# Operand sums cast one turn later, six blocks carried into the first block unit, and weight-conversion steps set by stage

## The chip, the core and the metric

The kernel runs on one core of a Trainium2 chip. The metric is device microseconds (us) of one execution; lower is better. The engines that matter here are PE (TensorE: matrix products, into PSUM), DVE (VectorE) and ACT (ScalarE), and SP, whose queue issues all the DMA of the stretch in question. Each engine runs its own instructions strictly in the order in which they stand in its program, and waits when the next one's inputs or buffers are not there yet.

## What is computed

Local attention with block summaries (8 heads, 2 batches, 768 positions), then a token and channel mixer, then a second channel mixer with a layer norm in front. The change touches the last two parts:

```python
u = x + h.transpose(0, 2, 1)                          # after the token mixer
x = u + np.maximum(u @ w_ch1, 0.0) @ w_ch2            # first layer:  512 -> 1536 -> 512
xn = (x - mu) / np.sqrt(var + 1e-06) * g_ln
out = x + np.maximum(xn @ w_ch1, 0.0) @ w_ch2         # second layer: 512 -> 2048 -> 512
```

All is in float32. Weights arrive as 64-bit numbers. They are decoded on the core to float32, and each float32 matrix is split in a high and a low part, so that a product is three matrix multiplications (high by high, high by low, low by high; `mm3`, lines 275 to 277).

## The kernel before

**Weight conversion.** The weights come in 62 pieces, called halves (512 columns of all 128 partitions each). A generator, `conversion`, handles one half after the other: an SP load into one of 3 stage buffers (L168), an absolute value on ACT (L115, tile `dec`), four bit operations on DVE (L129, L131, L133, L137), then the split: a cast on ACT for the high part and a subtraction on DVE for the low part. The first 30 halves stay in SBUF, in tiles called slots. The other 32 belong to the second layer: they are split into a spill buffer (tile `sp`, or `sps` for the sums of four blocks; casts on ACT at L186 to L190 and L250, subtractions on DVE at L210 to L220 and L255) and written back to DRAM by an SP DMA. There are two spill buffers, used in turn, so the cast of one spill waits until the write of the spill before the last one has landed. `convert_all(n)` advances the generator by n steps; a step is about one DVE operation.

**First layer.** The 1536 rows are taken in 4 groups of 3 row tiles and 12 chunks (key c = 3 to 14). A unit is one chunk of one group: `g3` (12 multiplications of 384 columns into a PSUM bank of the pool `ps_mm`, then ReLU: `ah` on ACT, L624, and `al` on DVE, L625) and, one unit later, `g4` (three blocks of three 512-column multiplications into the group's accumulators). There are 48 units, n = 0 to 47: first 24 for groups 0 and 1, then 24 for groups 2 and 3. After each unit the kernel before calls `convert_all(5)`. Background work runs between the blocks of `g4`: `start(1)` advances a background generator, `finish()` ends what was started. Both together are called a turn here. The transposition of the rows (`transpose_u`, tiles `tu` and `xt`) is such work. `ps_mm` has two banks, which `g3`, the transposes and the second layer's products share in turn.

**Operands of the second layer.** `prep_x` normalizes a row group (ACT, tile `xn`, L554), transposes it on PE (tile `tx`, L585), scales it on ACT (tile `f`), makes the sums T1 to T4 on DVE, and casts each operand into its high and low parts (`split`, L572 on ACT, L573 on DVE). Eight turns make the operands of one half of the rows. Those for the first half are made from n = 38 on, those for the second half in block units 2 to 5.

**Second layer.** 16 block units follow (`unit`, 8 for each half of the rows). Each makes seven products of block sums (k = 0 to 6, two `mm3` of 384 columns each, operands B11, T2, B21, T1, B22, T3, T4), combines them on DVE (tiles `sm`, `um`, `wm`, L686; the first is a copy on ACT, L696), applies ReLU (L677, L678) and leaves twelve second-matrix blocks (`second`), which the next unit places between its own products. The blocks that a unit gets are spread over its seven products: as many at each as are left, divided by the products left, rounded up. `step(k)` follows each product: it advances the conversion by 2 or 3 steps and runs background turns. Weights are loaded from DRAM into rings that lie in the slots of the first layer.

**What sets the order.** From n = 10 on, ACT's order is that of the code; from the block units on, PE's too. The order on DVE and SP, and on PE in the first layer, is made by a scheduler that places instructions by estimates of its own, so an edit in one place moves instructions in others.

## Time and profile before

| | |
|---|---|
| runs | 596.69, 599.54 and 600.32 us; median 599.54 us |
| profiled execution | 596.65 us, its span 594.5 us |
| PE busy | 569.3 us, 96% of the span |
| DVE busy | 407.8 us, 69% |
| ACT busy | 256.8 us, 43% |
| DMA | 121.07 MB, mean 204 GB/s |
[...]

The span runs from the first to the last instruction; 2.15 us of the execution lie around it. The profile has a line of 40 slices in which PE is almost always at 9 (90% or more), with lower digits in the attention part at the front and in slices 23 and 25 (327 to 342 us and 357 to 372 us). Durations of matmuls are modelled and overlap: what one multiplication occupies is read from the distance of two starts.

### The profile page before, as it was taken

The page shows a single profiled execution, that of the slowest core. Times are in us where ns is not written, and L with a number is a line of the kernel's source. Part 1 is how long each engine was busy: PE and PEld are TensorE (multiplying, and loading weights), DVE is VectorE, ACT ScalarE, POOL GpSimd, SP SyncE. Part 2 cuts the span into 40 slices and gives each one's busy share as a digit, 9 for nine tenths or more (in the row PEclk, how much of TensorE's full clock was granted, in tenths as well). Part 3 has the DMA queues.
Part 4 walks back from the last instruction along what each step waited for, and adds up shares of the span by engine and source line. Part 5 has one row for each costly group of instructions (what it writes and reads, how often), then busy time and mean ns, then how long its engine had stood idle before and what let it go on. Part 6 is the DMA issues. An engine that isn't in the chain of part 4 may idle for free.

```text
span 594.5 us, 9756 instructions
## 1 busy us (share of the span) xinstructions
PE 569.3 (96%) x3488; PEld 491.6 (83%) x3488; DVE 407.8 (69%) x992; ACT 256.8 (43%) x559; POOL 44.2 (7%) x78
## 2 busy tenths in 40 slices
PE   7878999999999999999999797999999999999997
PEld 3456777788999889999889686888889989898896
DVE  4799997995399799786799898854543644333334
ACT  3889888442144345243885334544311111111110
POOL 1555622000000000000000000000000000000000
PEclk8998999999999999999999898999999999999999
DMA  8999930344044467687589988865656775565412
GB/s 281 340 279 300 279 107 4 106 142 142 1 145 171 140 249 240 230 299 253 187 266 332 293 314 305 311 219 174 191 181 192 231 226 179 182 190 182 140 35 107
DMA packets 51206, 121.07 MB, mean 204 GB/s; under 512 B 5075, under 2 KB 11475, under 8 KB 51158
## 3 DMA queue, kind: packets, MB, share of 16 engines
q1 hardware_dynamic: 51152, 120.43, 62.2%
q8 instruction: 28, 0.46, 0.3%
q14 instruction: 20, 0.16, 0.1%
q10 hardware_dynamic: 6, 0.02, 0.0%
HBM read 94.21 MB, written 26.21 MB: 203 GB/s over the span
## 4 chain that ended last, share of the span: by engine, by line
PE 79%; DVE 7%; DMA 7%; ACT 5%; issue 1%; SPq 1%; ACTq 0%; DVEq 0%
PE acc_x L276 7%; PE acc_x L277 7%; PE acc_x L275 7%; PE m L275 6%; PE m L276 6%; PE m L277 6%; DMA stage<-in_wts_dram 4%; PE g L275 2%; DMA w2s<-sp 2%; PE g L277 2%; PE g L276 2%; ACT pr L391 2%; PE av L418 1%; DVE dec L133 1%; PE pt L398 1%
## 5 line engine op out<-in xcount | busy, mean ns | idle before, releaser
L276 PE MATMUL acc_x<-slot,ah 128*128 128x512 f32 x192 | 76.0, 396 | 0.0
L275 PE MATMUL acc_x<-slot,ah 128*128 128x512 f32 x192 | 75.9, 395 | 0.0
L277 PE MATMUL acc_x<-slot,al 128*128 128x512 f32 x192 | 75.9, 395 | 0.0
L677 ACT ACTIVATE ah<-sm 128x384 fp32r<-128x384 f32 x32 | 16.8, 524 | 109.4 <-DVE sm L686 109.4
L275 PE MATMUL m<-slot,slot 128*128 128x384 f32 x126 | 44.1, 350 | 1.1 <-ACT sm L696 0.4
L137 DVE SCALAR_TENSOR_TENSOR dec<-stage,dec 128x512 uint32<-128x512 uint32 x62 | 44.5, 718 | 0.5
L115 ACT ACTIVATE dec<-stage 128x512 f32<-128x512 f32 x62 | 41.6, 674 | 7.6 <-DMA stage<-in_wts_dram 7.6
L133 DVE SCALAR_TENSOR_TENSOR dec<-stage,dec 128x512 uint32<-128x512 uint32 x62 | 43.5, 702 | 0.6
L277 PEld LDWEIGHTS acc_x<-slot,al 128*128 128x128 f32 x192 | 36.3, 189 | 8.1
L276 PE MATMUL m<-slot,slot 128*128 128x384 f32 x126 | 43.0, 342 | 0.0
L277 PE MATMUL m<-slot,slot 128*128 128x384 f32 x126 | 43.0, 341 | 0.0
L276 PEld LDWEIGHTS acc_x<-slot,ah 128*128 128x128 f32 x192 | 36.5, 190 | 4.1
L275 PEld LDWEIGHTS acc_x<-slot,ah 128*128 128x128 f32 x192 | 36.5, 190 | 3.8
L391 ACT ACTIVATE pr<-sn,mn 128x120 f32<-128x120 f32 x96 | 30.6, 385 | 5.7 <-DVE mn L381 5.3
L686 DVE TENSOR_TENSOR um<-m,sm 128x384 f32<-128x384 f32 x16 | 8.9, 557 | 28.9 <-PE m L277 28.6
L129 DVE TENSOR_SCALAR dec<-dec 128x512 f32<-128x512 f32 x62 | 27.2, 441 | 2.0 <-ACT dec L115 2.0
L275 PEld LDWEIGHTS m<-slot,slot 128*128 128x128 f32 x126 | 24.0, 190 | 5.1 <-DVE um L686 1.3
L678 DVE SCALAR_TENSOR_TENSOR al<-sm,ah 128x384 fp32r<-128x384 f32 x32 | 17.8, 557 | 13.0 <-ACT ah L677 13.0
L131 DVE TENSOR_SCALAR dec<-dec 128x512 uint32<-128x512 uint32 x62 | 26.3, 424 | 0.4
L276 PEld LDWEIGHTS m<-slot,slot 128*128 128x128 f32 x126 | 24.0, 191 | 2.0
L361 PE MATMUL scores<-K,Q 64*64 64x120 f32 x384 | 16.4, 289 | 9.2 <-DVE mn L381 6.2
L686 DVE TENSOR_TENSOR sm<-m,sm 128x384 f32<-128x384 f32 x16 | 8.9, 555 | 23.3 <-PE m L277 23.3
(1392 smaller groups left out, 1490.4 us busy)
## 6 DMA issues: line engine op xcount, KB each, us to landing
stage<-in_wts_dram SPq DMA_DIRECT2D x62, 512.0 KB, 3.7
slot<-w1s SPq DMA_DIRECT2D x94, 256.0 KB, 3.0
slot<-w2s SPq DMA_DIRECT2D x32, 512.0 KB, 4.0
w1s<-sps SPq DMA_DIRECT2D x16, 512.0 KB, 3.6
w2s<-sp SPq DMA_DIRECT2D x16, 512.0 KB, 4.6
V<-in_v_dram SPq DMA_DIRECT2D x16, 306.0 KB, 7.7
extra<-w1s SPq DMA_DIRECT2D x18, 256.0 KB, 3.4
w1s<-sp SPq DMA_DIRECT2D x8, 512.0 KB, 4.1
```

Of the source, the lines that this page charges most:

```text
L115: nc.scalar.activation(m, self.raw[n][:, :, 1].bitcast(F32), AF.Abs)
L129: nc.vector.tensor_scalar(m, m, MAG_LO, MAG_HI, op0=ALU.max, op1=ALU.min)
L131: nc.vector.tensor_scalar(mi, mi, 3, 0x3FFFFFF8, op0=ALU.logical_shift_left, op1=ALU.bitwise_and)
L133: nc.vector.scalar_tensor_tensor(mi, t[:, :, 1], 0xC0000000, mi, op0=ALU.bitwise_and, op1=ALU.bitwise_or)
L137: nc.vector.scalar_tensor_tensor(mi, t[:, :, 0], 29, mi, op0=ALU.logical_shift_right, op1=ALU.bitwise_or)
L275: nc.tensor.matmul(out, lhs[0], rhs[0], start=first, stop=False)
L276: nc.tensor.matmul(out, lhs[0], rhs[1], start=False, stop=False)
L277: nc.tensor.matmul(out, lhs[1], rhs[0], start=False, stop=last)
L391: nc.scalar.activation(pr[:, u], sn[:, u], AF.Exp, bias=mn[:, u : u + 1], scale=-1.0)
L677: nc.scalar.activation(ah, x, AF.Relu)
L678: nc.vector.scalar_tensor_tensor(al, x, 0.0, f32(ah), op0=ALU.max, op1=ALU.subtract)
L686: add = lambda o, x, y: nc.vector.tensor_tensor(o, x, y, op=ALU.add)
```

## The change

Four edits.

1. `prep_x` gets one more turn in front, in which only the first normalization stands, and the casts of the sums T1 to T4 are kept in a list and made one turn later, after the next turn's scaling and normalization. Both preparations take nine turns instead of eight; the second is queued one block unit earlier, so that its first turn falls in block unit 1.
2. `g4` returns its three blocks as functions. The last unit (n = 47) doesn't run the blocks of chunk 13 but hands them on, together with those of chunk 14: block unit 0 gets six blocks instead of the three of chunk 14 that it ran behind its first product, and spreads them over its first six products.
3. The steps after a unit are 5 for n below 10, 6 for n = 10 to 23, 5 for n = 24 to 38 and 4 for n from 39; in the block units each product is followed by 2 steps instead of 2 and 3 in turn.
4. The weight loads for ring places 9 to 11 move from the first to the last product of block unit 0. In block unit 1, nine turns instead of eight.

```diff
 # prep_x
         self.normalize(2 * s + seq[0][2], seq[0][0] + 2 * seq[0][1])
-        f, t = {}, {}
+        yield
+        yield
+        f, t, wait = {}, {}, []
...
                 self.normalize(2 * s + ni, ne + 2 * nh)
+            for k, v in wait:
+                self.split(s, *k, v)
+            wait = []
...
-                self.split(s, "T1", e, t["T1"])
+                wait.append((("T1", e), t["T1"]))
...
-                self.split(s, "T3", e, t["T3"])
-                self.split(s, "T2", e, t["T2"])
+                wait.append((("T3", e), t["T3"]))
+                wait.append((("T2", e), t["T2"]))
...
-                self.split(s, "T4", e, t["T4"])
+                wait.append((("T4", e), t["T4"]))
             if n + 1 == len(seq):
+                for k, v in wait:
+                    self.split(s, *k, v)
 # g4
-        for j in range(GT):
-            s = slice(j * P, j * P + P)
...
+        return [lambda j=j: self.g4_tile(g, c, a, j, first, last) for j in range(GT)]
+
+    def g4_tile(self, g, c, a, j, first, last):
+        s = slice(j * P, j * P + P)
+        acc = self.acc[g % 2 * GT + j]
+        self.mm3(acc, (a[0][:, s], a[1][:, s]), self.half[2 * c + 1], first, last)
+        if last:
+            us = self.u[:, g * GT + j]
+            self.nc.vector.tensor_tensor(us, acc, us, op=ALU.add)
+        self.finish()
+        self.start(1)
 # run, first layer
             if (s, f, g) == (1, 5, 3):
-                later += [self.prep_x(0)] * 8
+                later += [self.prep_x(0)] * 9
...
-                self.g4(*prev)
+                blocks = self.g4(*prev)
+                if n == len(units) - 1:
+                    pending += blocks
+                else:
+                    for fn in blocks:
+                        fn()
...
-            self.convert_all(5)
+            self.convert_all(5 if n < 10 or 24 <= n < 39 else 6 if n < 24 else 4)
 # run, block units
-        pending = deque([lambda: self.g4(*prev)])
+        pending += self.g4(*prev)
...
-                if n == 0 and k == 0:
+                if n == 0 and k == 6:
                     for r in range(9, RING):
                         self.load_w1(r)
-                self.convert_all(2 + k % 2)
+                self.convert_all(2)
                 if n == 1 or n in range(2, 6) and k in (1, 5):
-                    for _ in range(2 if (n, k) == (1, 6) else 1):
+                    for _ in range(2 if n == 1 and k > 4 else 1):
...
-            if n == 2:
-                self.bg += [self.prep_x(1)] * 8
+                self.bg += [self.prep_x(1)] * 9
```

The order of the instructions moves in three places that the prediction speaks of. A row gives the line, the operation, the tile written and the tiles read.

**Place 1, ACT, where the first layer goes from groups 0 and 1 to groups 2 and 3.** `ah_('u', 1)_14` is the last ReLU of group 1, `ah_('u', 2)_3` the first of group 2, the `xt` casts empty the transposes of group 3. Before:

```order
L624 ACTIVATE ah_('u', 1)_14_2658<-g3_('u', 1)_14_2645 128x384
L514 CAST xt2_69<-tu_3_0_2665 128x384
L514 CAST xt2_69<-tu_3_1_2674 128x384
L186 CAST sp34_2687<-dec34_2597 128x2x256
L115 ACTIVATE dec36_2689<-stage36_2603 128x512
L624 ACTIVATE ah_('u', 2)_3_2712<-g3_('u', 2)_3_2699 128x384
L514 CAST xt2_69<-tu_3_2_2683 128x384
```

After:

```order
L631 ACTIVATE ah_('u', 1)_14_2687<-g3_('u', 1)_14_2674 128x384
L514 CAST xt2_69<-tu_3_0_2694 128x384
L514 CAST xt2_69<-tu_3_1_2703 128x384
L250 CAST sps1_0_2717<-sa1_2669 128x2x256
L250 CAST sps1_1_2719<-sb1_2670 128x2x256
L190 CAST sp36_2725<-dec36_2595 128x512
L115 ACTIVATE dec38_2727<-stage38_2627 128x512
L631 ACTIVATE ah_('u', 2)_3_2744<-g3_('u', 2)_3_2731 128x384
L514 CAST xt2_69<-tu_3_2_2712 128x384
```

The conversion stands one half and a half further on there. Between the two ReLUs, where one spill cast (`sp34`) stood, there now stand the two casts of sums (`sps1_0`, `sps1_1`) and behind them the next spill cast, `sp36`, which takes the buffer of `sps1_0`.

**Place 2, ACT, at the start of block unit 2.** `sm_2` is the copy that frees the PSUM bank of the unit's first product, `xn_2_0` the first normalization for the second half of the rows, `sd_3` a square root of the statistics. Before:

```order
L190 CAST sp57_4130<-dec57_3937 128x512
L115 ACTIVATE dec59_4132<-stage59_3963 128x512
L537 ACTIVATE sd_3_4139<-ve_3_4138 128x3
L696 COPY sm_2_4163<-m0_2_4155 128x384
L186 CAST sp58_4193<-dec58_4081 128x2x256
L115 ACTIVATE dec60_4195<-stage60_4108 128x512
L554 ACTIVATE xn_2_0_4199<-u_137,nb_2_4057,rs_2_4049 128x128 x3
L589 ACTIVATE f1_0_B11_4207<-tx_2_0_4203,gt_140 128x384
```

After:

```order
L190 CAST sp57_4132<-dec57_3921 128x512
L115 ACTIVATE dec59_4134<-stage59_3943 128x512
L537 ACTIVATE sd_3_4138<-ve_3_4137 128x3
L554 ACTIVATE xn_2_0_4152<-u_137,nb_2_4057,rs_2_4049 128x128 x3
L704 COPY sm_2_4166<-m0_2_4158 128x384
L591 ACTIVATE f1_0_B11_4201<-tx_2_0_4197,gt_140 128x384
L554 ACTIVATE xn_3_0_4203<-u_137,nb_3_4150,rs_3_4142 128x128 x3
```

`xn_2_0` moved from behind the spill cast `sp58` to a place in front of the copy `sm_2`; `sp58` moved behind the two of them and further back.

**Place 3, ACT, from the end of the first layer to block unit 0.** `ah_('u', 3)_14` is the last ReLU of the first layer, slots 5 to 9 hold the operands B22, T3, T2, B21 and T4, `sm_0` is the copy after the first product. Before:

```order
L589 ACTIVATE f0_1_B21_3741<-tx_0_3_3734,gt_140 128x384
L572 CAST slot8_1626<-f0_1_B21_3741 128x384
L572 CAST slot9_1627<-t0_1_T4_3745 128x384
L624 ACTIVATE ah_('u', 3)_14_3775<-g3_('u', 3)_14_3762 128x384
L250 CAST sps5_0_3790<-sa5_3758 128x2x256
L250 CAST sps5_1_3792<-sb5_3759 128x2x256
L696 COPY sm_0_3808<-m0_0_3800 128x384
```

After:

```order
L190 CAST sp52_3756<-dec52_3540 128x512
L115 ACTIVATE dec54_3758<-stage54_3590 128x512
L631 ACTIVATE ah_('u', 3)_14_3774<-g3_('u', 3)_14_3761 128x384
L591 ACTIVATE f0_1_B21_3789<-tx_0_3_3785,gt_140 128x384
L572 CAST slot6_1624<-t0_1_T3_3745 128x384
L572 CAST slot7_1625<-t0_1_T2_3746 128x384
L572 CAST slot8_1626<-f0_1_B21_3789 128x384
L572 CAST slot9_1627<-t0_1_T4_3797 128x384
L704 COPY sm_0_3811<-m0_0_3803 128x384
```

Three operand casts (slots 6, 7 and 9) and that of the last transposed block (slot 8) now stand behind the last ReLU, and a spill cast, `sp52`, in front of it; the two casts of sums that stood between are gone from here, they come two units earlier.

## Rows read from the trace of the kernel before

**Rows 1.** Stretches of core 0: us, busy time by engine, clock, DMA share.

```profile
core 0: us, PE busy (x) PEld busy (x) DVE busy (x) ACT busy (x) POOL busy (x), PEclk, DMA share, GB/s
120.00:320.00 200.00, 200.00 (x1024) 180.49 (x1023) 158.78 (x330) 92.47 (x186) 0.00 (x0) 1.00 0.58 196
320.00:366.00 46.00, 39.13 (x174) 33.18 (x174) 42.67 (x104) 19.63 (x41) 0.00 (x0) 0.93 0.93 319
366.00:585.00 219.00, 218.63 (x1090) 196.09 (x1089) 103.40 (x194) 53.62 (x112) 0.00 (x0) 1.00 0.58 184
```

**Rows 2.** PE in order of time: start, us, line, tiles; idle before and releaser.

```profile
321.43 0.33 PE L275 MATMUL m<-slot 128*128 128x384 f32 x1
...
328.26 0.44 PE L275 MATMUL m<-slot,slot 128*128 128x384 f32 x1 [0.35 <-DVE sm L686]
...
331.54 0.44 PE L275 MATMUL m<-slot 128*128 128x384 f32 x1 [0.90 <-DVE sm L686]
...
334.21 0.49 PE L275 MATMUL m<-slot,extra 128*128 128x384 f32 x1 [1.35 <-DVE um L686]
...
336.10 0.63 PE L275 MATMUL acc_x<-slot,ah 128*128 128x512 f32 x1
...
338.73 0.44 PE L275 MATMUL m<-slot,extra 128*128 128x384 f32 x1 [0.27 <-DVE um L686]
...
341.88 0.45 PE L275 MATMUL m<-slot,slot 128*128 128x384 f32 x1 [0.43 <-ACT sm L696]
...
346.85 0.34 PE L275 MATMUL m<-slot,slot 128*128 128x384 f32 x1
...
347.91 0.39 PE L275 MATMUL acc_x<-slot,ah 128*128 128x512 f32 x1
...
349.29 0.34 PE L275 MATMUL m<-slot,slot 128*128 128x384 f32 x1
...
361.58 1.24 PE L585 MATMUL tx<-ident,xn 128*128 128x128 f32 x3 [3.53 <-ACT xn L554]
362.48 0.67 PE L275 MATMUL m<-slot,slot 128*128 128x384 f32 x1
...
364.55 0.63 PE L275 MATMUL acc_x<-slot,ah 128*128 128x512 f32 x1
...
366.24 0.34 PE L275 MATMUL m<-slot,slot 128*128 128x384 f32 x1
```

**Rows 3.** ACT in order of time, at the start of block unit 2.

```profile
357.90 0.46 ACT L696 COPY sm<-m 128x384 f32<-128x384 f32 x1
359.96 0.62 ACT L186 CAST sp<-dec 128x512 fp32r<-128x512 f32 x1 [1.59 <-DMA w2s<-sp]
360.48 0.66 ACT L115 ACTIVATE dec<-stage 128x512 f32<-128x512 f32 x1
361.05 1.25 ACT L554 ACTIVATE xn<-u,nb,rs 128x128 f32<-128x128 f32 x3
```

**Rows 4.** DVE in order of time, end of the first layer and block unit 0.

```profile
320.24 0.55 DVE L625 SCALAR_TENSOR_TENSOR al_('u', 3)_14_3776<-g_('u', 3)_14_3762,ah_('u', 3)_14_3775 128x384 fp32r<-128x384 f32 x1
...
333.59 0.56 DVE L686 TENSOR_TENSOR um<-m,um 128x384 f32<-128x384 f32 x1
```

**Rows 5.** ACT in order of time, the turn to groups 2 and 3.

```profile
217.08 0.48 ACT L514 CAST xt<-tu 128x384 fp32r<-128x384 f32 x1 [0.55 <-PE tu L510]
...
220.68 0.49 ACT L624 ACTIVATE ah_('u', 2)_3_2712<-g_('u', 2)_3_2699 128x384 fp32r<-128x384 f32 x1 [2.03 <-PE g_('u', 2)_3_2699 L277]
```

**Rows 6.** PE and DVE at the same turn.

```profile
222.10 0.40 PE L275 MATMUL acc_('u', 2)_0_2765<-slot,ah_('u', 2)_3_2712 128*128 128x512 f32 x1
...
217.69 0.55 DVE L515 TENSOR_TENSOR xt<-tu,xt 128x384 fp32r<-128x384 f32 x1
```

**Rows 7.** DVE and ACT around 250 us: two spilled sums and the next spill.

```profile
250.88 0.69 DVE L255 TENSOR_TENSOR sps<-sa,sps 128x512 fp32r<-128x512 f32 x1
...
254.43 0.62 ACT L190 CAST sp<-dec 128x512 fp32r<-128x512 f32 x1 [3.06 <-DMA w1s<-sps]
...
255.52 0.47 ACT L624 ACTIVATE ah_('u', 3)_5_3053<-g_('u', 3)_5_3040 128x384 fp32r<-128x384 f32 x1
```

**Rows 8.** DVE and ACT around 321 us: the same pair, and the next spill.

```profile
321.04 0.69 DVE L255 TENSOR_TENSOR sps<-sa,sps 128x512 fp32r<-128x512 f32 x1
...
325.76 0.62 ACT L190 CAST sp<-dec 128x512 fp32r<-128x512 f32 x1 [2.58 <-DMA w1s<-sps]
```

More of the change, by code (lines that the diff above doesn't have):

```diff
@@ L628, in g4 @@
     def g4(self, key, c, a, first, last):
-        nc = self.nc
         g = key[1]
@@ L634, in g4 @@
                 self.acc[i] = self.ps_acc.tile([P, 512], F32, tag=f"acc{i}", name=f"acc_{key}_{j}")
-        for j in range(GT):
-            s = slice(j * P, j * P + P)
-            acc = self.acc[g % 2 * GT + j]
-            self.mm3(acc, (a[0][:, s], a[1][:, s]), self.half[2 * c + 1], first, last)
-            if last:
-                us = self.u[:, g * GT + j]
-                nc.vector.tensor_tensor(us, acc, us, op=ALU.add)
-            self.finish()
-            self.start(1)
+        return [lambda j=j: self.g4_tile(g, c, a, j, first, last) for j in range(GT)]
[8 more added lines that the diff above has]
+        self.start(1)
     def ring_w1(self, n):
@@ L923, in run @@
         order = ctx.enter_context(ExitStack())
-        later = deque()
+        later, pending = deque(), deque()
         for n, (s, f, g) in enumerate(units):
```

## The prediction

> **What bounds the kernel now.** I read four views: the busy time by stretch, PE in order of time, ACT and DVE in order of time around PE's waits, and the order of before and after. The first shows that PE sets the time: it is busy for 200.00 of 200 us up to 320 us and for 218.63 of 219 us from 366 us on, at granted clock 1.00. Only between 320 and 366 us does it stand idle, 39.13 of 46 us busy, with DVE at 42.67 us and clock 0.93 [rows 1]. So no edit can gain anything outside these 46 us, unless it takes work from PE, which none does; and anything that makes PE wait elsewhere is lost at once.
>
> What these 46 us lose follows from PE's own rows [rows 2]. From the first product of block unit 0 (321.43) to the fourth of unit 2 (366.24) are 44.81 us. Undisturbed, a product takes 1.06 us (346.85 to 347.91) and a block 0.69 (347.91 to 349.29 holds two). The stretch holds 17 products (7, 7 and 3) and 21 blocks (3 in unit 0, 12 in unit 1, 6 in unit 2), 18.0 and 14.5 us, and one group of transposes, an estimated 0.4. That is 32.9, so **11.9 us are lost**. Six waits hold 6.83 of it: 0.35, 0.90, 1.35, 0.27, 0.43 and 3.53. [...] From 334.21 to 338.73 stand one product and two blocks, 2.44 undisturbed, and the wait of 0.27; from 361.58 to 366.24 the transposes, a product and two blocks, 2.84 undisturbed. They take 4.52 and 4.66, so the lower level costs 1.8 us each time, 3.6 together. The remaining 1.5 is some 0.25 at each wait, for the pipeline to drain and fill.
>
> [...]
>
> **What the edits do to this stretch.** *The last wait.* The 3.53 us at 361.58 end with ACT's `xn`. ACT has it behind a spill cast that itself waits 1.59 us for a write to land: cast 359.96, absolute value 360.48, `xn` 361.05 [rows 3]. After the change `xn_2_0` stands in front of `sm_2` (357.90) and the spill cast behind both, so it can be done about 2 us before PE wants it: statistics for it are ready, since edit 1 gives it a turn of its own in front. The wait goes (3.53), the low clock behind it (1.8) and the refill (0.25): 5.6 us. What is late next is `sm_2`, by up to `xn`'s 0.57 of ACT; PE has two blocks (1.38) there as cover.
>
> *The waits for DVE.* Between `al` of the last chunk (320.24) and the `um` that frees the bank for unit 1 (333.59) DVE runs 27 instructions, 0.49 each, without a pause worth the name [rows 4]. It is the bound there: PE's work over it is 7 products and 3 blocks, 9.5 us, against 13.3. Edit 2 lays three more blocks between the products: 2.1 us of cover, taken from n = 47, where PE was not waiting. Edit 3 brings the conversion some eight DVE operations ahead by the end of the first layer, and takes 14 instead of 17 steps in a block unit; in the order DVE has 110 instead of 121 instructions from `al` of the last chunk to the third `al` of unit 0's results. Up to the `um` named it is only 26 for 27. So of the 13.3 us some 12.8 remain, against 11.6 of PE work: the wait at unit 1's first product shrinks from 1.35 plus those ahead of it to 1.1 to 2.2, without certainty that the clock holds. Against it, place 3 adds a wait at unit 0's second product, whose operand T2 (slot 7) is now cast behind the last ReLU and behind `f`: 0.4, up to 2 if the write in front of `sp52` lands late. I leave 2.2 us in the stretch (1.8 at unit 1, 0.4 at T2); the waits of units 1 and 2 (0.27, 0.43) go with the eleven DVE instructions fewer (11 × 0.49 = 5.4). **Gain 11.9 − 2.2 = 9.7 us**; bounds 5.6 (the last wait alone) and 11.9.
>
> **What they cost elsewhere.** *Place 1, near 222 us.* Before, ACT writes `xt` of group 3's second transposes at 217.08, then a spill cast and an absolute value, and then waits 2.03 us for PE before the first ReLU of group 2 at 220.68 [rows 5]; PE's block on it starts at 222.10 without a wait [rows 6]. After, two casts of sums and `sp36` stand there, and `sp36` takes the buffer of the first sum, so it waits until that sum has gone to DRAM. The same pair stands near 250 us: DVE's subtraction starts at 250.88, and the next spill cast, after 3.06 us of waiting for the write, at 254.43, that is 3.55 later; the ReLU behind it starts 1.09 after that [rows 7]. Where DMA is busier, the subtraction at 321.04 is followed by the spill cast at 325.76, 4.72 later [rows 8]. At 250 us PE lost nothing, since the ReLU there was not yet needed; at the turn it is, for PE's next block reads it.
>
> [...]
>
> Now the sum. The subtraction for `xt` is at 217.69 [rows 6]; DVE has it, 0.55, and some small statistics ahead of the subtraction of the first sum, which I put at 218.75. Plus 3.55 is 222.3 for `sp36`, plus 1.09 is 223.4 for the ReLU, against 220.68; plus the 1.42 from ReLU to block (220.68 to 222.10) is 224.8. PE would stand 2.7 us at most, and 1.9 if the sum starts 0.4 earlier and the ReLU is followed at once by the block; I take **2.4**, with 4 as upper bound (4.72 instead of 3.55) and 0 as lower (if the scheduler's DVE order lets the sum go ahead of group 3's work). Whether the clock falls behind a single wait of that size no row shows: behind 3.53 and behind three waits of 2.60 in six us it did, behind 0.35 and 0.90 it did not. I charge half of 1.8, **0.9**.
>
> *Costed at nothing.* The casts put off by a turn (edit 1) lie in stretches in which PE doesn't wait [rows 1]; they are the same casts, and what they hide behind is PE's 1.38 us of blocks at each product. What they cost without it is place 3's T2. The nine later loads (edit 4) are needed in the middle of unit 1, some ten us after their issue; they go down SP's queue behind the spill writes. Steps taken from the block units cost nothing as long as the last spilled weights are in DRAM before unit 4 reads them, and the conversion is only five operations behind at unit 2.
>
> **The sum**, on the profiled execution's own time: 596.65 − 9.7 + 2.4 + 0.9 = **590.2**. That execution stands at the low end of the runs (596.69), 2.9 us under their median; I carry half of that, 1.4, and get **591.5**. About 1%, 6 us, is what a measurement of this kernel can tell from no change; the forecast lies just past it.
>
> **Rivals.** *A, the forecast*: most waits go, one new one at 222 us; 588 to 593.5.
>
> *B, the turn costs nothing*: ACT's write lands in time, or DVE does the sum early. For it: 2.03 us of idle ACT stand in front of the ReLU [rows 5]. Against it: 3.55 + 1.09 is more than what lies between 217.69 and 220.68. Then 596.65 − 9.7 = 587.0, or with the whole 11.9 584.8; with the median's 1.4, 586 to 588.4.
>
> *C, the waits only move*: place 3's `sp52` waits for the sums' write as at 325.76, and the ReLU `ah` of the last chunk with it, T2 comes 2 us late and the clock falls there, in unit 0 and at 222 us. Then only the last wait's 5.6 is gained, and 2.4 + 1.8 are paid, with up to 2 more at T2: 595.3 to 597.3, or with the median's 1.4 up to 598.7.
>
> *D, slower*: six steps a unit put spill casts directly in front of ReLUs on ACT throughout n = 10 to 23, not at the turn alone. In each such pair a cast waits for the write 2.58 to 3.06 us [rows 7, 8]; `g3` of a unit gives its ReLU about one unit of slack, so PE pays only when the wait starts late in it. If it pays 2.4 at each of the turn and three other places, 9.6 is paid against 9.7 gained and from the fifth on the change loses: with lowered clock behind each, 600 to 606. Against it: PE waits nowhere before 320 us now although such pairs are there already [rows 1, 7].
>
> **How the numbers follow.** Chances: A 0.50, B 0.12, C 0.30, D 0.08. The likeliest gives 591.5, its own range 588 to 593.5. Leaving out D and the lower part of B leaves 586 to 598. Faster by over 1% (under 593.5) takes A nearly whole, with 0.42, and B's 0.12 less a little for runs that lie high: 0.52. Within 1% takes the rest of A and C less a little: 0.40. Slower: D, 0.08.
>
> **What would show it.** In the trace of the changed kernel: no wait of PE for `xn` at unit 2, and product times of 1.06 us there; one wait of PE for ACT's ReLU of group 2's first chunk near 222 us, with ACT's `sp36` waiting for `w1s<-sps` just ahead; waits of 0.4 us at T2 and 1 to 2 us at unit 1's first product, on DVE; clock 0.97 or more between 320 and 366 us. The prediction is wrong in its gain if PE still waits over 4 us in this stretch, wrong in its cost if the turn shows no wait or more than 4 us, and wrong altogether if PE waits at several chunks between n = 10 and 23.

## The result and the profile after

The changed kernel takes 591.64 us (median of 8 runs) against 599.45 us before (8 runs). The timed ratio is 0.9882, 95% interval 0.9852 to 0.9912; the plain ratio of the two medians, 0.9870, lies inside that interval. The forecast was 591.5.

Busy time of the changed kernel in the stretches of [rows 1] (the columns are those; the last stretch ends 3 us earlier, since the program does):

```profile
120.00:320.00 200.00, 197.84 (x1009) 178.69 (x1010) 160.23 (x332) 89.08 (x178) 0.00 (x0) 1.00 0.58 197
320.00:366.00 46.00, 43.45 (x221) 38.95 (x220) 45.02 (x109) 23.58 (x51) 0.00 (x0) 1.00 0.92 325
366.00:582.00 216.00, 215.41 (x1074) 193.02 (x1073) 103.19 (x193) 53.45 (x112) 0.00 (x0) 1.00 0.59 186
```

PE, which was never idle between 120 and 320 us, now loses 2.16 us there. Between 320 and 366 us it is busy for 43.45 us instead of 39.13, and the clock is 1.00 instead of 0.93. DVE is busier than before, 45.02 of 46 us. (The changed program is some 5 us later there. With the stretch moved along, 324.97 to 370.97 us, PE is busy for 43.30 and DVE for 45.12 us, and the clock is 1.00 again.)

PE of the changed kernel in order of time: three marks (last chunk of group 1, third chunk of group 2, last chunk of group 3), its waits between them and after, and the first transpose in unit 2, to set beside [rows 2]:

```profile
215.82 0.33 PE L275 MATMUL g_('u', 1)_14_2674<-xt,slot 128*128 128x384 f32 x1
...
227.44 0.50 PE L275 MATMUL acc_('u', 2)_0_2797<-slot,ah_('u', 2)_3_2744 128*128 128x512 f32 x1 [2.08 <-ACT ah_('u', 2)_3_2744 L631]
...
232.04 0.34 PE L275 MATMUL g_('u', 2)_5_2821<-xt,slot 128*128 128x384 f32 x1
...
322.22 0.34 PE L275 MATMUL g_('u', 3)_14_3761<-xt,slot 128*128 128x384 f32 x1
...
326.43 0.44 PE L275 MATMUL m<-slot 128*128 128x384 f32 x1 [1.62 <-ACT f_B L591]
...
339.24 0.44 PE L275 MATMUL m<-slot,extra 128*128 128x384 f32 x1 [0.93 <-DVE um L694]
...
359.90 0.49 PE L587 MATMUL tx<-ident,xn 128*128 128x128 f32 x3
360.19 0.44 PE L275 MATMUL m<-slot,slot 128*128 128x384 f32 x1
...
587.28 0.39 PE L277 MATMUL acc_x<-slot,al 128*128 128x512 f32 x1
```

The wait of 3.53 us for `xn` is gone: the transpose at 359.90 starts without one. Three waits of some size are left: a new one of 2.08 us for the first ReLU of group 2, a new one of 1.62 us at unit 0's first product, and 0.93 us at unit 1's. The next longest after 200 us is 0.31 us, at the last product of unit 2.

The same marks before:

```profile
212.73 0.33 PE L275 MATMUL g_('u', 1)_14_2645<-xt,slot 128*128 128x384 f32 x1
...
226.63 0.34 PE L275 MATMUL g_('u', 2)_5_2789<-xt,slot 128*128 128x384 f32 x1
...
590.52 0.39 PE L277 MATMUL acc_x<-slot,al 128*128 128x512 f32 x1
```

So the **turn** (group 1's last chunk to group 2's third) takes 16.22 us instead of 13.90, and the **rest** (from there to the last multiplication) 355.24 instead of 363.89. Together that is 6.33 us less. The two profiled executions are only 3.27 us apart (593.38 and 596.65 us), because the part in front of all the changes was 3.1 us longer in the one of after: the first layer (first multiplication of unit n = 0) starts at 108.42 us there and at 105.34 before. In the fourteen traces of this study that start lies between 105.17 and 109.12 us, whatever the kernel; the edits begin behind it, at n = 10. I therefore compare traces by turn and rest, and whole kernels by the timed ratios. Each kernel has one trace. The turn repeats well: in the eight traces without a wait it takes 13.86 to 13.90 us. How well the rest repeats for one and the same kernel no run shows, so differences of a few tenths in it are not to be read.

### The profile page after: what moved, and what is told of

It is laid out like the page before. It is cut to its first block, busy times and chain, and to the rows that moved or that the text cites. A ratio compares the mean times of both kernels' runs of the same rounds, so it can differ in the third digit from the quotient of the medians.

```text
span 591.5 us, 9753 instructions
## 1 busy us (share of the span) xinstructions
PE 565.5 (96%) x3483; PEld 490.5 (83%) x3488; DVE 410.1 (69%) x992; ACT 256.2 (43%) x559; POOL 42.7 (7%) x78
## 4 chain that ended last, share of the span: by engine, by line
PE 78%; DMA 8%; DVE 6%; ACT 5%; issue 1%; POOL 0%; SPq 0%; ACTq 0%; DVEq 0%; POOLq 0%
PE acc_x L276 7%; PE acc_x L277 7%; PE acc_x L275 7%; PE m L275 6%; PE m L276 6%; PE m L277 6%; DMA stage<-in_wts_dram 2%; DMA w1s<-sps 2%; PE g L275 2%; PE g L277 1%; ACT pr L391 1%; PE g L276 1%; DMA VT<-in_vt_dram 1%; PE av L418 1%; PE pt L398 1%
## 5 line engine op out<-in xcount | busy, mean ns | idle before, releaser
L275 PE MATMUL m<-slot,slot 128*128 128x384 f32 x126 | 43.2, 343 | 0.3
L276 PE MATMUL m<-slot,slot 128*128 128x384 f32 x126 | 42.7, 339 | 0.0
L277 PE MATMUL m<-slot,slot 128*128 128x384 f32 x126 | 42.6, 338 | 0.0
L129 DVE TENSOR_SCALAR dec<-dec 128x512 f32<-128x512 f32 x62 | 28.4, 461 | 2.7 <-ACT dec L115 2.7
L131 DVE TENSOR_SCALAR dec<-dec 128x512 uint32<-128x512 uint32 x62 | 27.7, 447 | 0.6
L381 DVE CUSTOM_DVE_ANT_0 sn<-scores,mask 128x120 f32<-128x120 f32 x96 | 21.7, 274 | 5.1 <-PE scores L361 3.1
```

The source lines that it names most:

```text
L129: nc.vector.tensor_scalar(m, m, MAG_LO, MAG_HI, op0=ALU.max, op1=ALU.min)
L131: nc.vector.tensor_scalar(mi, mi, 3, 0x3FFFFFF8, op0=ALU.logical_shift_left, op1=ALU.bitwise_and)
L275: nc.tensor.matmul(out, lhs[0], rhs[0], start=first, stop=False)
L276: nc.tensor.matmul(out, lhs[0], rhs[1], start=False, stop=False)
L277: nc.tensor.matmul(out, lhs[1], rhs[0], start=False, stop=last)
L381: self.ttr[n] = nc.vector.tensor_tensor_reduce(sn[:, u], ps[:, u % 2, u // 2, :NK], self.mask[:, mv], scale=-SCALE, scalar=3e38, op0=ALU.a ...
```

## The experiments

All times in us. Turn and rest come from the trace's start times of the marks above; "to unit 1" is from the last chunk of group 3 to unit 1's first product, "units 1, 2" from there to unit 2's second transposes. The ratio is timed, to the kernel before. "To unit 1" holds one group of transposes more (0.4 us) in the kernels with nine turns, since in those with eight it runs ahead of the mark.

| kernel | turn | rest | to unit 1 | units 1, 2 | ratio, 95% interval |
|---|---|---|---|---|---|
| before | 13.90 | 363.89 | 16.96 | 38.65 | 1 |
| changed | 16.22 | 355.24 | 17.02 | 30.12 | 0.9882 (0.9852 to 0.9912) |
| u_steps | 13.90 | 363.15 | 19.29 | 33.73 | 0.9941 (0.9923 to 0.9960) |
| u_turn | 17.73 | 354.87 | 15.46 | 31.01 | 0.9912 (0.9882 to 0.9943) |
| u_blocks | 17.75 | 355.13 | 17.15 | 30.13 | 0.9900 (0.9863 to 0.9937) |
| turn_late | 13.86 | 355.75 | 16.81 | 30.46 | 0.9857 (0.9823 to 0.9892) |
| steps_alone | 17.66 | 355.84 | 16.00 | 31.57 | 0.9905 (0.9877 to 0.9934) |
| turn_alone | 13.87 | 362.79 | 19.62 | 33.74 | 0.9955 (0.9932 to 0.9978) |
| u_steps_units | 16.20 | 359.58 | 17.52 | 33.06 | 0.9977 (0.9945 to 1.0009) |
| late_eight | 13.88 | 355.65 | 15.46 | 31.02 | 0.9813 (0.9769 to 0.9857) |
| late_eight_few | 13.86 | 353.22 | 14.52 | 30.00 | 0.9843 (0.9812 to 0.9874) |
| u_casts_loads | 17.63 | 357.52 | 19.66 | 30.00 | 0.9931 (0.9907 to 0.9955) |
| late_eight_blocks | 13.89 | 355.42 | 16.29 | 30.40 | 0.9877 (0.9829 to 0.9925) |
| steps_only_few | 13.89 | 353.56 | 14.78 | 30.05 | 0.9848 (0.9812 to 0.9884) |

My theory A was the prediction's: edit 1 takes away the wait for `xn`, the blocks and the fewer steps take away the waits for DVE, and edit 3 pays for it at the turn. The rivals gave the gain to one edit alone, or said that a wait only moves. What was expected of each run stands above its result, with the names of the theory and its rival.

### Edit 3 undone (u_steps)

```diff
-            self.convert_all(5 if n < 10 or 24 <= n < 39 else 6 if n < 24 else 4)
+            self.convert_all(5)
...
-                self.convert_all(2)
+                self.convert_all(2 + k % 2)
```

> The changed kernel with edit 3 undone: five steps after every unit and 2 or 3 in turn in the block units, edits 1, 2 and 4 kept. On ACT the first ReLU of group 2 then stands behind one spill cast that waits for no sum, and xn_2_0 still stands ahead of sm_2 and of the spill cast. Theory A (the price of edit 3 is the turn to group 2, its gain the DVE work taken from the block units): the wait of 2.1 us near 227 us goes, and the waits on DVE in block units 0 and 1 (2.8 us in the changed kernel) grow by 1 to 3 us, so that the two nearly cancel: 0 to 2 us more than the changed kernel, and about 5 to 8 us less than the kernel before. Rival R (the relief of DVE by fewer steps carries most of the gain): the waits of unit 1 and the lower clock behind them return, 4 to 6 us, and the result is 2 to 4 us slower than the changed kernel.

The ratio rises by 0.0059, 3.5 us: rival R holds, but without the lower clock that it expected (the granted clock is 1.00 from 318 to 400 us). The turn is back at 13.90, so its price is edit 3's alone. But the rest takes 363.15, almost what it took before, though edits 1, 2 and 4 are all in place. PE's waits in it, from unit 1 on:

```profile
338.92 0.44 PE L275 MATMUL m<-slot,extra 128*128 128x384 f32 x1 [1.43 <-DVE um L694]
...
342.26 0.44 PE L275 MATMUL m<-slot,extra 128*128 128x384 f32 x1 [0.65 <-DVE um L694]
...
359.28 0.44 PE L275 MATMUL m<-slot,slot 128*128 128x384 f32 x1 [0.67 <-DVE um L694]
...
362.59 0.55 PE L587 MATMUL tx<-ident,xn 128*128 128x128 f32 x3 [0.62 <-ACT sm L704]
363.49 0.44 PE L275 MATMUL m<-slot,slot 128*128 128x384 f32 x1 [0.35 <-DVE um L694]
...
374.45 0.44 PE L275 MATMUL m<-slot,extra 128*128 128x384 f32 x1 [1.30 <-DVE um L694]
...
391.92 0.45 PE L275 MATMUL m<-slot,slot 128*128 128x384 f32 x1 [0.86 <-DVE um L694]
```

None of them is for `xn`: ACT had that ready in time. What PE no longer waits for there it waits for at DVE's sums: in small pieces over units 1 to 3, and 2.3 us more in front of unit 1 (19.29 against 16.96).

### Edit 1's turn of its own undone (u_turn)

```diff
-        yield
-        yield
...
-                later += [self.prep_x(0)] * 9
+                later += [self.prep_x(0)] * 8
...
-                    for _ in range(2 if n == 1 and k > 4 else 1):
+                    for _ in range(2 if (n, k) == (1, 6) else 1):
...
-                self.bg += [self.prep_x(1)] * 9
+            if n == 2:
+                self.bg += [self.prep_x(1)] * 8
```

> The changed kernel without edit 1's turn of its own for the first normalization (eight turns again, the second preparation queued in unit 2); the casts put off by one turn, edits 2, 3 and 4 are kept. Theory A as forecast: the turn is what removes the wait of 3.5 us for xn at unit 2, so it comes back with the lower clock behind it, 5 to 6 us slower than the changed kernel. Rival S (what delayed xn was the spill cast, and fewer steps alone move that away): in this kernel's order ACT has xn right behind sm_2 with the spill cast further back, PE waits 1 us or less for it, and the time is within 1.5 us of the changed kernel. At 227 us nothing changes, 2.1 us of waiting.

Rival S holds. The rest is 354.87 us, no longer than the changed kernel's 355.24. ACT at the start of unit 2:

```profile
360.31 0.20 ACT L537 ACTIVATE sd<-ve 128x3 f32<-128x3 f32 x1 [1.41 <-DVE ve L536]
360.43 0.46 ACT L702 COPY sm<-m 128x384 f32<-128x384 f32 x1
360.78 1.27 ACT L554 ACTIVATE xn<-u,nb,rs 128x128 f32<-128x128 f32 x3
362.47 0.58 ACT L589 ACTIVATE f_B<-tx,gt 128x384 f32<-128x384 f32 x1 [0.42 <-PE tx L585]
```

`xn` follows the copy directly, where in [rows 3] a spill cast with its wait for a write stood between: edit 3 by itself has moved the conversion, and that cast stands elsewhere. No wait of PE is listed there, but the transposes follow `xn` piece by piece and take 0.87 us up to the next product, where the changed kernel's take 0.29 (359.90 to 360.19):

```profile
361.33 1.10 PE L585 MATMUL tx<-ident,xn 128*128 128x128 f32 x3
362.20 0.41 PE L275 MATMUL m<-slot,slot 128*128 128x384 f32 x1
```

PE waits 2.04 us at the turn, as in the changed kernel, but the turn takes 17.73 us instead of 16.22 in this execution (granted clock 0.84 from 221 to 232 us; the clock at the turn, below). Its timed ratio, 0.9912 of four runs, has an interval that overlaps with the changed kernel's; how often the clock fell in the runs without a trace isn't shown.

### Edit 2 undone (u_blocks)

```diff
-                blocks = self.g4(*prev)
-                if n == len(units) - 1:
-                    pending += blocks
-                else:
-                    for fn in blocks:
-                        fn()
+                for fn in self.g4(*prev):
+                    fn()
...
-        pending += self.g4(*prev)
+        pending = deque([lambda: [fn() for fn in self.g4(*prev)]])
```

> The changed kernel with edit 2 undone: the last two chunks' blocks run as before, three in n = 47 and three in one piece behind unit 0's first product. Theory A: 2.1 us of cover go from unit 0, PE's waits on DVE up to unit 1's first product (1.2 us in the changed kernel) become 2 to 4 us, with the lower clock behind them in part: 1 to 4 us slower than the changed kernel. Rival T (DVE's own chain sets when unit 1 can start, wherever the blocks lie): the waits add up to the same, within 0.5 us of the changed kernel.

Rival T holds: the rest is 355.13 against 355.24. The wait for `f` at unit 0's first product is gone, since the blocks of chunk 13 run in front of it. In its place stand 1.11 us and 1.63 us for DVE, so that unit 1 starts 17.15 instead of 17.02 us after the mark:

```profile
334.64 0.44 PE L275 MATMUL m<-slot,slot 128*128 128x384 f32 x1 [1.11 <-DVE wm L694]
...
338.64 0.44 PE L275 MATMUL m<-slot,extra 128*128 128x384 f32 x1 [1.63 <-DVE um L694]
```

### Three steps moved behind n = 24 (turn_late)

```diff
-            self.convert_all(5 if n < 10 or 24 <= n < 39 else 6 if n < 24 else 4)
+            self.convert_all(3 if n == 23 else 8 if n == 24 else 5 if n < 10 or 24 <= n < 39 else 6 if n < 24 else 4)
```

> The changed kernel with three of the six steps after n = 23 moved behind n = 24 (3 and 8 instead of 6 and 5): on ACT the first ReLU of group 2 then stands right behind the two casts of sums, and the spill cast sp36 behind that ReLU and two more casts of the transposes; all else stands as in the changed kernel. Theory A (PE's wait near 227 us is sp36's wait for the write of the first sum, nothing else): the 2.1 us go with the 0.25 behind them, 2.3 us faster than the changed kernel, other stretches unchanged. Rival U (the wait only moves, to the next product of group 2 or 3, since everything behind sp36 waits for the same write): under 0.5 us gained.

Theory A holds. ACT of the changed kernel at the turn:

```profile
220.79 0.62 ACT L250 CAST sps<-sa 128x512 fp32r<-128x512 f32 x1
221.31 0.62 ACT L250 CAST sps<-sb 128x512 fp32r<-128x512 f32 x1
225.82 0.62 ACT L190 CAST sp<-dec 128x512 fp32r<-128x512 f32 x1 [3.89 <-DMA w1s<-sps]
226.35 0.66 ACT L115 ACTIVATE dec<-stage 128x512 f32<-128x512 f32 x1
226.91 0.48 ACT L631 ACTIVATE ah_('u', 2)_3_2744<-g_('u', 2)_3_2731 128x384 fp32r<-128x384 f32 x1
```

And with the steps moved:

```profile
221.16 0.62 ACT L250 CAST sps<-sb 128x512 fp32r<-128x512 f32 x1
224.16 0.49 ACT L631 ACTIVATE ah_('u', 2)_3_2738<-g_('u', 2)_3_2725 128x384 fp32r<-128x384 f32 x1 [2.38 <-PE g_('u', 2)_3_2725 L277]
...
226.50 0.63 ACT L190 CAST sp<-dec 128x512 fp32r<-128x512 f32 x1
```

The ReLU now waits for PE, and no longer PE for it; by the time the spill cast comes, at 226.50, the write has landed. The turn takes 13.86 us. Of the 2.36 us gained the rest gives 0.51 back, so that 1.85 are left. The one wait that has grown is that at the last product of unit 2, from 0.31 to 0.71 us, for a sum of DVE.

### Edit 3 alone, and edit 1 alone, on the kernel before (steps_alone, turn_alone)

The diffs are the parts of the change that are numbered 3 and 1 (1 with the nine turns in block unit 1).

> Edit 3 alone, on the kernel before (no turn of its own, casts, blocks and loads as before). In its order xn_2_0 follows sm_2 directly, the spill cast sp58 having moved back. Theory A1 (edits 1 and 3 each by themselves take the spill cast out from in front of xn, and the lower step count takes DVE work from the block units): PE's wait of 3.5 us for xn goes with the lower clock behind it, the 2.1 us near 227 us come, and PE's waits on DVE in units 0 and 1 are 1 to 4 us; 3 to 6 us less than the kernel before. Rival R1 (without the six blocks as cover DVE's waits and the lower clock at unit 1 stay as they were): less than 3 us gained, and the waits up to unit 1's first product again 2.6 us or more.

Theory A1 holds for edit 3. The rest takes 355.84, 8.05 us less than before, of the 8.65 us that the whole change gains. The only waits of over 0.2 us that are left after 200 us are these, and the product behind the second is slow (1.13 us to the next row, which is its second half, instead of some 0.5):

```profile
224.06 0.80 PE L275 MATMUL acc_('u', 2)_0_2797<-slot,ah_('u', 2)_3_2744 128*128 128x512 f32 x1 [1.96 <-ACT ah_('u', 2)_3_2744 L626]
...
336.83 0.69 PE L275 MATMUL m<-slot,extra 128*128 128x384 f32 x1 [1.87 <-DVE um L689]
...
337.96 0.52 PE L275 MATMUL m<-slot,extra 128*128 128x384 f32 x1
```

> Edit 1 alone, on the kernel before: nine turns, the casts of sums one turn later, the second preparation queued in unit 1; steps, blocks and loads as before. Theory A1: xn_2_0 stands ahead of sm_2, so the 3.5 us and the 1.8 of lower clock go, and nothing is paid near 222 us; 4 to 6 us less than the kernel before. Rival R2 (the stretch is bound by DVE, and what is not waited for at xn is waited for at the next um or sm, as the kernel without edit 3 shows: its waits from unit 1 to unit 4 add up to some 6 us): less than 3 us gained, with waits on DVE instead in units 1 to 4.

Rival R2 holds. The timed gain is 0.45%, 2.7 us; in the trace the rest is 1.10 us shorter. The 3.53 us for `xn` are gone here too: units 1 and 2 take 33.74 us instead of 38.65. But unit 1 starts 2.66 us later, with waits of 1.03, 1.60, 0.68 and 1.35 us on DVE in front of it, and another 1.30 us are lost behind the second transposes of unit 2. The loss in front has a count: from `al` of the last chunk to the `um` that frees the bank for unit 1, DVE now runs 32 instructions in 15.84 us, where it ran 27 in 13.35 before ([rows 4]). The ninth turn has put the last operands' sums and subtractions behind the last ReLU.

### Only the block units' half of edit 3 undone (u_steps_units)

```diff
-                self.convert_all(2)
+                self.convert_all(2 + k % 2)
```

> The changed kernel with the second half of edit 3 undone: 2 or 3 steps in turn behind the products of a block unit instead of 2, the steps of the first layer as changed. Theory R (the three steps fewer in every block unit are what takes DVE's waits away): the waits of 0.4 to 1.3 us in units 1 to 4 return, and the result is 3 to 5 us slower than the changed kernel. Rival V (the operations done ahead by the end of the first layer are what counts): within 1.5 us of the changed kernel. In both the 2.1 us near 227 us stay.

Theory R holds. The rest is 4.34 us longer, 359.58. With all of edit 3 undone it was 7.91 longer, which leaves 3.6 for the steps done ahead in the first layer; that half wasn't undone by itself.

### The turn put right and eight turns (late_eight)

This is the diff of turn_late and that of u_turn together.

> The changed kernel with two things put right: three of the steps after n = 23 moved behind n = 24, and edit 1's turn of its own taken back (eight turns), so that the last transposed group of the first half is scaled before the last ReLU. From the runs of each alone: no wait near 227 us (2.3 us less than the changed kernel), no wait of 1.6 us for f at unit 0's first product (1.6 less), 0.3 to 0.9 more around unit 2, where xn follows sm_2. 2 to 3.5 us faster than the changed kernel. Rival W (the two gains do not add, since PE arriving earlier at unit 0 waits longer for DVE there): no faster than the kernel with the steps moved alone, 1.9 us under the changed kernel in its trace.

By the trace rival W holds. Unit 1 starts 1.35 us sooner after its mark than with the steps moved alone (15.46 against 16.81; some 0.4 of it only because one more group of transposes now runs ahead of the mark), but the rest takes 355.65 against 355.75. The wait at the last product of unit 2 has grown from 0.71 to 0.99 us, and units 1 and 2 take 0.56 more, about what the slower transposes cost under "u_turn". The timed ratios, 0.9813 and 0.9857, have intervals that overlap.

### Fewer steps in block units 0 to 2 (late_eight_few)

```diff
-                self.convert_all(2)
+                self.convert_all(1 if n < 3 else 2)
```

(on top of late_eight)

> The kernel with the steps moved behind n = 24 and eight turns, and in block units 0 to 2 one step behind each product instead of two (two from unit 3 on). Theory R (DVE's load in the block units sets their waits): the waits on DVE that the kernel without this has left, 0.56, 0.78 and 0.99 us, go, and the stretches from unit 1 to unit 4 lose 1 to 2 us more; 2 to 3.5 us faster than that kernel, some 13 us less than the kernel before. Rival X (the work only comes later and delays weights that units 3 to 5 read from DRAM, or the operands of the second half): PE waits for a ring place or an operand there, and the time is the same or longer.

In the trace theory R holds: the rest falls by 2.43 us to 353.22, and the waits of 0.78 and 0.99 us become none and 0.52. Busy time between 318 and 372 us, first of late_eight, then of this kernel:

```profile
318.00:372.00 54.00, 51.46 (x257) 45.44 (x256) 51.06 (x123) 25.06 (x53) 0.00 (x0) 1.00 0.94 321
```

```profile
318.00:372.00 54.00, 52.93 (x269) 47.51 (x268) 44.58 (x105) 22.14 (x49) 0.00 (x0) 1.00 0.87 292
```

DVE has 18 instructions less there and, for the first time, idle time: it is busy for 44.58 of 54 us. The times don't show the 2.4 us: 0.9843 against 0.9813, with overlapping intervals, in separate series. Which of the two is faster stays open.

### Casts at once, loads early (u_casts_loads)

```diff
-                wait.append((("T1", e), t["T1"]))
+                self.split(s, "T1", e, t["T1"])
...
-                if n == 0 and k == 6:
+                if n == 0 and k == 0:
```

(T2, T3 and T4 likewise)

> The changed kernel with the casts of the sums T1 to T4 made at once again, as before, and the loads of ring places 9 to 11 (edit 4) back behind the first product; the turn of its own, blocks and steps stay as changed. Forecast: both are hidden, within 0.5 us of the changed kernel from group 1's last chunk to the end. Rival Y (the later casts take DVE and ACT work out from in front of the ReLUs at the start of the second layer): waits at unit 0's first products grow, 1 us slower or more.

It is 2.6 us later at unit 1, through a wait that says something else than I asked. The block of chunk 13 waits 2.35 us for the load of a ring place:

```profile
330.87 0.53 PE L276 MATMUL acc_('u', 3)_1_2972<-slot,ah_('u', 3)_13_3723 128*128 128x512 f32 x1 [2.35 <-DMA slot<-w1s]
```

In this kernel the three early loads write over the second-matrix weights of chunks 12 to 14, and the blocks held back by edit 2 read those of 13 and 14 only afterwards. Those blocks compute with other weights here, so this kernel no longer computes the same function. Edit 4 thus belongs to edit 2 and isn't a tuning of its own. Whether the casts are hidden the run doesn't show cleanly, since a wait of 2.35 us and the lower clock behind it (a product takes 1.92 us, 331.63 to 333.55; granted clock 0.97 from 318 to 372 us) can cover them. What speaks for it: from `al` of the last chunk to `um` DVE runs 26 instructions in both kernels, without the 2.35 us unit 1 starts within 0.3 us of the changed kernel, and units 1 and 2 take 30.00 against 30.12.

### The blocks once more, without the wait for f (late_eight_blocks)

This is late_eight with the diff of u_blocks.

> The kernel with the steps moved behind n = 24 and eight turns, with edit 2 undone (blocks as before). With the wait for f at unit 0's first product out of the way, theory A expects the six blocks' cover to count: waits up to unit 1's first product 1.3 us with them, 2 to 3.5 us without, 1 to 2 us slower than the kernel with them. Rival T (DVE's chain alone decides): within 0.5 us.

Rival T holds again, and now one sees why. PE's waits from unit 0 on, first of late_eight, then without its blocks:

```profile
322.31 0.45 PE L275 MATMUL m<-slot,slot 128*128 128x384 f32 x1 [0.56 <-ACT sm L702]
...
333.21 0.44 PE L275 MATMUL m<-slot,extra 128*128 128x384 f32 x1 [0.78 <-DVE um L692]
...
365.71 0.45 PE L275 MATMUL m<-slot,extra 128*128 128x384 f32 x1 [0.99 <-DVE um L692]
```

```profile
330.36 0.44 PE L275 MATMUL m<-slot,slot 128*128 128x384 f32 x1 [0.54 <-DVE wm L692]
...
334.36 0.44 PE L275 MATMUL m<-slot,extra 128*128 128x384 f32 x1 [1.65 <-DVE um L692]
...
365.78 0.44 PE L275 MATMUL m<-slot,extra 128*128 128x384 f32 x1 [0.53 <-DVE um L692]
```

With the blocks unit 1 starts 0.83 us sooner; by the end of unit 2 all of it is given back: 0.8 us where the first transposes of unit 2 follow `xn` piece by piece, as in u_turn, and 0.46 at unit 2's last product (0.99 instead of 0.53 us for `um`). The rest is 355.65 with them and 355.42 without. In both kernels unit 1's first product starts 0.05 us after the `um` that frees its bank ends.

### Steps and nothing else (steps_only_few)

The kernel before with the step tables of turn_late and late_eight_few.

> The kernel before with nothing but a table of steps: as edit 3 in the first layer, three of those after n = 23 moved behind n = 24, and one step behind each product in block units 0 to 2, two from unit 3 on; preparation, casts, blocks and loads as before. Theory R (steps are the whole matter: they take the spill casts out from in front of xn and of the first ReLU of group 2, and DVE's work out of the block units): no wait near 222 us, none for xn, DVE's waits in units 0 to 3 under 1.5 us together; from group 1's last chunk to the end within 1.5 us of the kernel that has these steps and eight turns (367.1 us), 588 to 590 us in all. Rival A2 (the six blocks or the later casts are needed for unit 1's first product): a wait of 1.5 to 2.5 us there, with or without the lower clock behind it, 2 to 4 us slower than that.

Theory R holds. These are the only waits of PE of over 0.2 us after 200 us:

```profile
334.25 0.44 PE L275 MATMUL m<-slot,extra 128*128 128x384 f32 x1 [0.68 <-DVE um L689]
...
365.31 0.44 PE L275 MATMUL m<-slot,extra 128*128 128x384 f32 x1 [0.52 <-DVE um L689]
```

The rest takes 353.56 us, 10.33 less than before and 0.34 more than with preparation, casts, blocks and loads changed as well; the turn takes 13.89. Its time is 589.33 us, a ratio of 0.9848 (0.9812 to 0.9884): faster than the kernel before, and not to be told from the changed kernel by the timed intervals, which overlap. By the trace it is 4.01 us ahead of that one.

## Why the prediction was right, and where it was not

**The bound** was read rightly: PE outside 320 to 366 us gained nothing, and the one place where PE was made to wait elsewhere cost its full length.

**The price of the turn** was forecast as 2.4 us and is 2.32 (16.22 less 13.90). Step by step it is less exact. The changed trace lies 3.09 us later than that of before at the turn. Less that, the subtraction of the first sum stands at 218.78 (forecast 218.75), `sp36` at 222.73 (222.3) and the ReLU at 223.82 (223.4). The subtraction, in the changed trace's own time, is this row:

```profile
221.87 0.68 DVE L255 TENSOR_TENSOR sps<-sa,sps 128x512 fp32r<-128x512 f32 x1
```

From it to the spill cast are 3.95 us, between the 3.55 of [rows 7] and the 4.72 of [rows 8]; less the 0.68 of the subtraction itself, 3.27 us. The block follows the ReLU by 0.53 us, not by 1.42 as in [rows 5, 6]; these two errors cancel.

**The clock at the turn** was charged with half of 1.8 us, because no row decided it. The 1.8 us, the price of the lower level of the clock in the prediction, are worked out from [rows 2] for a product and the two blocks behind it. The products alone, behind the third and the sixth wait, take 1.89 and 2.07 us there instead of 1.06, at a granted clock of 0.57 and 0.50 instead of the 1.00 of 120 to 320 us:

```profile
334.21:336.10 1.89, 1.89 (x6) 1.89 (x7) 0.54 (x1) 1.28 (x3) 0.00 (x0) 0.57 0.83 261
362.48:364.55 2.07, 2.07 (x8) 2.07 (x9) 1.46 (x3) 1.69 (x5) 0.00 (x0) 0.50 0.91 313
```

It didn't fall in the changed kernel's trace (1.00 from 200 to 240 us). Of the six traces with this wait (1.93 to 2.08 us) it fell in four (0.84 from 221 to 232 us in u_turn, u_blocks and steps_alone, 0.96 from 200 to 240 us in u_casts_loads): their turn takes 17.63 to 17.75 us, against 16.20 and 16.22 in the other two, 1.4 to 1.6 us more. As an expectation half was fair; in the trace that the sum is compared with, the 0.9 us were not paid.

**The gain** was forecast as 9.7 us and is 8.65. All of it lies in units 1 and 2 (30.12 us instead of 38.65); unit 1 starts no sooner after the mark than before (17.02 against 16.96, of which 0.4 are the transposes that ran ahead of the mark before). Of its parts:

- *The wait for xn* went with all that hangs on it, as forecast, but **the step that named its cause failed**. I gave it to edit 1, since `xn_2_0` moved ahead of `sm_2`. The runs show that edit 3 alone removes it too (steps_alone, u_turn), since fewer steps put another operation of the conversion there. I had both moves in the order and credited one. Edit 1 alone brings 1.10 us in the trace, not 5.6 (turn_alone): it gains 4.91 in units 1 and 2, but its ninth turn puts five more DVE instructions in front of unit 1, which costs most of the 2.66 lost there, and 1.30 are lost behind.
- *The waits at the start of the block units*: the place was wrong. I expected 0.4 us at the second product, for T2. It is 1.62 us at the first, for `f`. The last transposed group takes a bank of `ps_mm`, which the product needs. Edit 1's ninth turn puts the `f` that empties it behind the last ReLU, and that ReLU stands behind `sp52`, which waits 0.77 us for a write:

```profile
324.35 0.62 ACT L190 CAST sp<-dec 128x512 fp32r<-128x512 f32 x1 [0.77 <-DMA w1s<-sps]
324.88 0.66 ACT L115 ACTIVATE dec<-stage 128x512 f32<-128x512 f32 x1
325.44 0.47 ACT L631 ACTIVATE ah_('u', 3)_14_3774<-g_('u', 3)_14_3761 128x384 fp32r<-128x384 f32 x1
325.81 0.57 ACT L591 ACTIVATE f_B<-tx,gt 128x384 f32<-128x384 f32 x1
```

  I had these rows in the order (place 3) and read in them only whose operand was late, not whose bank. With 0.93 us at unit 1 the waits come to 2.55 us where 2.2 were left.
- *The blocks' 2.1 us of cover* were worth nothing in either pair of kernels (355.24 against 355.13, 355.65 against 355.42). The step that failed is that cover for PE shortens a stretch which DVE bounds. It lets PE run ahead, and ACT's `xn` and DVE's sums hold it up in unit 2 (late_eight); in the changed kernel it is held up in unit 0 already, for `f`. That DVE bounds the stretch was read rightly: from `al` of the last chunk to `um` it runs 26 instructions in 12.69 us, where 12.8 were forecast. Only fewer instructions shorten it: 20 in 10.48 us in late_eight, 18 in 9.06 in late_eight_few.
- *The steps* were sized as eleven instructions off DVE, with the units' later waits their only gain. They are the change: undoing them loses 7.91 of the 8.65 us. The count of 110 for 121 was also put at the wrong place: in the traces it ends at the last `al` of unit 2; at the third `al` of unit 0 it is 28 for 29.
- *Casts and loads* show no cost in the changed kernel's trace, as forecast (the loads are three, not nine); but the later loads are a need of edit 2, which I had not seen.

**To the median** I carried 1.4 us; the profiled execution of after lay 1.7 us above its median (593.38 against 591.64), that of before 2.8 below. The sum on the trace's own scale was 6.4 us of gain against 6.33 measured from mark to mark; the medians are 7.8 apart. That the sums met so closely is in part luck: the gain was forecast 1.05 us too large, and the 0.9 us charged for the clock, which were not paid, made that good. That 591.5 met 591.64 owes the rest to the offsets of the two executions. **The rivals**: B and D didn't occur. Of C the wait behind `sp52` came about, at 1.62 us. It did not take the gain away, since DVE had less to do: with edit 3 undone nearly all of the gain is lost (u_steps).

## What to carry to other kernels

When an engine in order is made to wait by work that a step count places, the first thing to vary is the count, at the one unit where the collision is: three steps moved by one unit gained 2.36 us of PE's time at the turn, and 1.85 in all. When several edits each seem to remove the same wait, undo each and make each alone; here one table of numbers held nearly all of the gain, and with that table in place the rest of the change added 0.3 to 1.0 us in the traces (steps_only_few against late_eight_few, steps_alone against the changed kernel and u_turn), no more than single traces can tell. Cover for the engine that waits gained nothing here, where the engine it waits for was busy nearly all the time, 45 of 46 us; taking work from that engine did.

## What was not expected of the hardware

The same wait of PE, 1.93 to 2.08 us at the same place, was followed by a lower granted clock in four traces and by none in two. From 60 us ahead of the turn up to the wait, PE runs the same 356 multiplications in the same order in all six, so the difference isn't one of PE's program. Busy time between 221 and 232 us, first of the changed kernel, then of the one with edit 2 undone:

```profile
221.00:232.00 11.00, 8.92 (x47) 7.76 (x46) 10.75 (x25) 4.98 (x11) 0.00 (x0) 1.00 0.61 216
```

```profile
221.00:232.00 11.00, 8.95 (x39) 7.94 (x38) 9.25 (x23) 4.93 (x10) 0.00 (x0) 0.84 0.64 234
```

PE is busy equally long in both, but gets through 47 multiplications in the one and 39 in the other. (Taken at the same distance from the turn's start as the second row, 223.26 to 234.26 us, the changed kernel's stretch holds 48, at clock 1.00.) So the price of such a wait is 2.3 us in some executions and 3.7 to 3.9 in others. What decides between them the traces don't show. A product was slow in steps_alone away from the turn too: behind the wait of 1.87 us at unit 1 half a product takes 1.13 us, against 0.53 undisturbed. The other surprise was the spread of the first 105 us, some 4 us from execution to execution, as large as most differences that were to be measured here.
